# Smaller TensorE matmuls in a recurrent attention kernel: every step padded to 1024 TensorE instructions

## The chip, the core and the metric

The kernel runs on one core of a Trainium2 chip. The core has five engines with instruction streams of their own: TensorE (matmul; the profile calls it PE and its weight loads PEld), VectorE (DVE), ScalarE (ACT), GpSimd (POOL) and SyncE (SP, which here only issues transfers). Transfers run on 16 DMA engines. Data lies in SBUF (128 partitions); matmul results go to PSUM, eight banks of 128 x 512 float32. The metric is the device time of one execution in microseconds (us). Before the change it is 2299.75 us, the median of three runs (2299.54 to 2310.22).

## What is computed

```python
def _A_ref(x, mem0, Wq, Wk, Wv, Wo, seg_len):       # x: (1, 2048, 1024), seg_len 32, 32 heads of 128
    ...
    mem = mem0                                       # 8 memory rows
    for s in range(n_seg):                           # 64 segments
        h = jnp.concatenate([mem, xs], axis=1)       # 8 + 32 rows
        q, k, v = (jnp.einsum('btd,dhe->bhte', h, W) for W in (Wq, Wk, Wv))
        scores = jnp.where(mask, jnp.einsum('bhqe,bhke->bhqk', q, k) * scale, -1e9)
        o = jnp.einsum('bhqk,bhke->bhqe', softmax(scores), v)
        o = jnp.einsum('bhte,hed->btd', o, Wo)
        mem = o[:, :M, :]                            # the first 8 rows are the next segment's memory
        outs.append(o[:, M:, :])
    ...
def _B_ref(x, w_gate, w_up, w_down):
    return _gelu(x @ w_gate) * (x @ w_up) @ w_down
g = sigmoid((x * gate_w).sum(-1, keepdims=True))
out = g * _A_ref(...) + (1 - g) * _B_ref(...)        # bfloat16
```

The 64 segments depend on each other through `mem`, so attention is a chain of 64 steps. The feed-forward part does not depend on it.

## The kernel before

The program first transposes `x` and starts the first projections, then runs the 64 steps of the recurrence (to about 1632 us), and then does the output projection of the rows that no later step needs and the feed-forward part.

In a step, a projection works with only 32 rows: the 8 memory rows and the first 24 rows of the segment. The other 8 rows of a segment depend on nothing earlier, so they are projected for four segments at once ("fill"). A projection piece multiplies a 128 x 32 block of the rows (the weights of the array) by a 128 x 2048 piece of `Wk`, `Wq` or `Wv`. It is issued as four matmuls of 512 columns, each on its own 32 columns of the array and its own 32 partitions of one PSUM bank; the four run side by side. A projection of 16 heads (half of all heads, `u` is 0 or 1) is eight pieces, so 32 matmuls. The weights do not fit into SBUF in full: some pieces share a slot, and `spent` issues the load of the next piece for a slot behind the matmuls that used it up.

The order of all work is written out by hand. `walk` lists the pieces in the order `k0, (second half of the old step's o1), q0, v0, k1, q1, o0, v1, (first half of o1)`, where 0 and 1 are the two halves of the heads. `plan(s)` hangs the other work of a step before certain pieces with `on(m, r, n, ...)`. TensorE executes its stream in exactly this order. Semaphores are derived from reads and writes by `_Prog`; an operation that has to wait for several things gets separate wait instructions ahead of it.

What the change touches and the prediction names:

- `mask` puts the causal mask into the bank of the scores by a matmul of the identity with the mask (L687). It is issued twice in a step, behind the transposes (`trans`, L673) of `q`.
- `scores` (L700) adds the 32 score matmuls; VectorE and ScalarE do the softmax and VectorE transposes the result into `tAB`.
- `attend(u)` multiplies by `v`: `f` is 16 matmuls with the 32 rows' `vA` (L729), `f2` four matmuls with the 8 rows' `vB` (L737). Then ScalarE and VectorE copy the result to `oT`. `attend(ua)` stands behind `q1`, before `o0`; `attend(ub)` stands behind `v1`.
- `fill(m, u, b)` gives eight functions, one for each piece of a projection of the other rows (L841). A step has up to two such projections: `f1` in parts of 3, 3 and the rest around `v1` and `attend(ub)`, `f2` four pieces before and four pieces behind `next_mem(s, 0)`.
- A step without a second fill calls `warm(5)` and `warm(2)` there: matmuls whose result nobody reads (L851).
- `fold` (VectorE) and `next_mem` (two transposes, L825, and a VectorE copy into `hT`) make the next step's memory rows. `next_mem(s, 0)` gives what the first pieces of the next step's `k0` read.
- `o0` (L787) and `o1` (L804) are the output projection of the step.

In the steady part a step has 955 to 979 TensorE instructions, when each matmul is counted as a weight load and a matmul, and each separate wait as one.

## Time and profile before

| what | value |
|---|---|
| median of three runs | 2299.75 us |
| profiled execution | 2308.1 us, span 2306.3 us |
| granted TensorE clock in it | 0.983 |
| TensorE matmuls in the program | 33852 |
| TensorE instructions, matmuls counted twice and with 484 waits and a few others | 68192 |
| recurrence, 125 to 1632 us | 1507 us, TensorE busy 1395.27 us, DMA share 0.93, 333 GB/s |
| the rest, 1632 to 2306 us | 674 us, TensorE busy 661.52 us, DMA share 0.42, 137 GB/s |

A line of the profile's groups reads: line of the kernel, engine, operation, output tile <- input tiles, shapes, count, then busy time and mean duration, then the idle time of the engine just before these instructions and what ended it. "issue" as the thing that ended it means that the profile shows nothing that the engine waited for. A line of a timeline begins with start and length in microseconds; its idle time stands in brackets at the end. Matmuls that run side by side overlap, so mean durations of one matmul are longer than the distance from start to start. The profile shows TensorE's instruction stream as a DMA queue of its own kind, "instruction".

### The profile page before, as it was taken

The numbers are of one execution on the slowest core, as the hardware profiler recorded it, in microseconds if no ns is written. First come the engines' busy times: TensorE is split into PE (matmuls) and PEld (weight loads), VectorE is DVE, ScalarE is ACT, GpSimd is POOL, SyncE is SP. The second block draws the span as 40 slices with busy tenths as digits, with TensorE's granted clock in tenths as the row PEclk, the third lists the DMA queues.
The fourth block names the chain that finished last, engine by engine and source line by source line (L and its number), as shares of the span: only waits on it lengthen the run. The fifth ranks groups of instructions, "written<-read, shape, count | busy, mean of one in ns | idle before, by whom it ended". The sixth has DMA issues, their size and how long they took to land.

```text
span 2306.3 us, 74586 instructions
## 1 busy us (share of the span) xinstructions
PE 2119.9 (92%) x33852; PEld 1048.7 (45%) x33852; DVE 1028.8 (45%) x2440; ACT 541.4 (23%) x1111; POOL 423.7 (18%) x821
## 2 busy tenths in 40 slices
PE   4598999999999999999999999998899999999999
PEld 2244444444444444444444444444464444444444
DVE  3343444454444444544444444454316446163462
ACT  1122222222222222222222222221113123032130
POOL 4422212222222222222222222221100000000000
PEclk8799999999999999999999999999899999999999
DMA  9989999898998999999989899999964440903520
GB/s 375 354 298 327 334 341 358 321 354 320 327 330 325 340 336 316 344 325 355 332 325 354 312 331 341 317 340 324 342 204 143 150 151 10 291 20 125 172 87 19
DMA packets 237579, 638.34 MB, mean 277 GB/s; under 512 B 22440, under 2 KB 91304, under 8 KB 230480
## 3 DMA queue, kind: packets, MB, share of 16 engines
q1 hardware_dynamic: 213440, 596.58, 72.4%
q0 software_dynamic: 13888, 26.31, 3.5%
q10 hardware_dynamic: 9936, 10.69, 1.4%
q8 instruction: 266, 4.36, 0.8%
q14 instruction: 49, 0.40, 0.0%
HBM read 596.85 MB, written 36.63 MB: 275 GB/s over the span
## 4 chain that ended last, share of the span: by engine, by line
PE 70%; DMA 19%; issue 4%; DVE 4%; ACT 2%; POOL 1%; ACTq 0%; SPq 0%; POOLq 0%
PE pb L771 23%; PE pb L1077 15%; DMA sl<-in_A_Wv_dram 7%; PE pb L1131 5%; PE pb L841 5%; PE pb L804 4%; PE pb L787 4%; PE pb L673 3%; DMA qkr<-qk_scr 3%; PE pb L1027 3%; PE pb L1112 2%; PE pb L851 2%; DMA wall<-wg_scr 2%; DMA xr_scr<-xr 1%; DMA o_scr<-oRc 1%
## 5 line engine op out<-in xcount | busy, mean ns | idle before, releaser
L771 PE MATMUL pb<-sl,hT 128*32 128x512 bf16 x12288 | 778.4, 383 | 28.8 <-issue 16.9
L771 PEld LDWEIGHTS pb<-sl,hT 128*32 128x32 bf16 x12288 | 337.5, 97 | 331.6 <-issue 50.8
L841 PE MATMUL pb<-sl,hR 128*32 128x512 bf16 x3072 | 225.3, 392 | 4.1 <-issue 3.2
L1077 PE MATMUL pb<-xT,wg 128*128 128x512 bf16 x896 | 211.7, 379 | 0.7
L1077 PE MATMUL pb<-xT,wu 128*128 128x512 bf16 x896 | 211.7, 379 | 0.0
L804 PE MATMUL pb<-wall,oT 128*32 128x256 bf16 x4056 | 150.9, 275 | 22.9 <-issue 8.5
L787 PE MATMUL pb<-wall,oT 128*32 128x512 bf16 x2048 | 152.4, 387 | 17.1 <-issue 9.5
L656 ACT ACTIVATE kS<-pb 128x512 bf16<-128x512 f32 x127 | 75.8, 597 | 384.3 <-PE pb L771 364.9
L815 DVE COPY part<-pb 64x256 f32<-64x256 f32 x128 | 54.0, 422 | 247.9 <-PE pb L804 246.9
L754 POOL COPY oRc<-oT 128x128 bf16<-128x128 bf16 x128 | 96.4, 753 | 359.2 <-DVE oT L659 357.0
L1131 PE MATMUL pb<-wd,GT 128*128 128x512 bf16 x672 | 146.0, 379 | 1.7 <-DMA wd<-in_B_w_down_dram 1.7
L1085 ACT ACTIVATE s<-pb 128x512 f32<-128x512 f32 x112 | 66.8, 596 | 311.9 <-PE pb L1077 311.9
L708 ACT ACTIVATE E<-pb 128x320 bf16<-128x320 f32 x128 | 55.9, 437 | 352.9 <-DVE pb L707 352.9
L1077 PEld LDWEIGHTS pb<-xT,wg 128*128 128x128 bf16 x896 | 87.2, 98 | 108.0 <-DVE GT L1093 3.7
L1077 PEld LDWEIGHTS pb<-xT,wu 128*128 128x128 bf16 x896 | 87.7, 98 | 105.7
L804 PEld LDWEIGHTS pb<-wall,oT 128*32 128x32 bf16 x4056 | 100.6, 96 | 74.9 <-ACT oT L656 25.9
L1086 DVE SCALAR_TENSOR_TENSOR tp<-s,pb 128x512 f32<-128x512 f32 x112 | 77.0, 687 | 124.2 <-ACT s L1085 124.0
L659 DVE CAST oT<-pb 128x160 bf16<-128x160 f32 x256 | 76.5, 320 | 111.7 <-PE pb L737 111.7
L659 DVE COPY kT<-pb 128x512 bf16<-128x512 bf16 x128 | 54.4, 425 | 159.8 <-PE pb L673 159.5
L880 POOL COPY kT<-qkr 128x128 bf16<-128x128 bf16 x128 | 37.3, 291 | 466.3 <-DVE kT L659 222.6
L841 PEld LDWEIGHTS pb<-sl,hR 128*32 128x32 bf16 x3072 | 82.3, 98 | 70.7 <-issue 20.8
L1090 DVE SCALAR_TENSOR_TENSOR tp<-tp,pb 128x512 f32<-128x512 f32 x112 | 77.1, 688 | 78.6 <-ACT tp L1089 78.6
(100 smaller groups left out, 2286.8 us busy)
## 6 DMA issues: line engine op xcount, KB each, us to landing
sl<-in_A_Wv_dram SPq DMA_DIRECT2D x128, 1024.0 KB, 10.8
wall<-wg_scr SPq DMA_DIRECT2D x53, 1536.0 KB, 9.2
sl<-in_A_Wk_dram SPq DMA_DIRECT2D x64, 1024.0 KB, 5.9
sl<-in_A_Wq_dram SPq DMA_DIRECT2D x64, 1024.0 KB, 9.0
wall<-wo_scr SPq DMA_DIRECT2D x120, 512.0 KB, 6.0
wd<-in_B_w_down_dram SPq DMA_DIRECT2D x42, 1024.0 KB, 5.4
sl<-in_A_Wv_dram SPq DMA_DIRECT2D x75, 512.0 KB, 11.1
wall<-in_A_Wo_dram SPq DMA_DIRECT2D x41, 512.0 KB, 7.9
```

The source lines that it names most:

```text
L656: op("act", lambda e: e.activation(o, i, ACTF.Copy), rd=rd, wr=wr)
L659: op("dve", lambda e: e.tensor_copy(o, i), rd=rd, wr=wr, after=after)
L673: ins = e.transpose(PBV[bank][:, j * 128:(j + 1) * 128], st[:, j * 128:(j + 1) * 128], ident[:, :])
L754: op("pool", lambda e: e.tensor_copy(oRc[:, :, 16 * u:16 * u + 16].rearrange("p c x -> p x c"), oT[:, :, :, 32:40].rearrange("p g j c -> p ...
L771: ins = e.matmul(PB[bk][32 * g:32 * g + 32, :], lhsT=h[:, i, :], rhs=w[:, g * 512:(g + 1) * 512], start=(n == 0), stop=(n == 7))
L787: ins = e.matmul(PB[XO][32 * g:32 * g + 32, :], lhsT=oT[:, j, x, 0:32], rhs=wall[:, na:nb + 1:nb - na, c:c + 256], start=(n == 0 and hp == 0),
L804: ins = e.matmul(PB[XO][32 * g:32 * g + 32, 256 * b:256 * b + 256], lhsT=oT[:, j, x, 0:32], rhs=w[:, c:c + 256], start=False, stop=(n % 4 ...
L841: ins = e.matmul(PB[b][32 * g:32 * g + 32, :], lhsT=h[:, k[2], :], rhs=w[:, g * 512:(g + 1) * 512], start=(n == 0), stop=(n == 7))
L1077: ins = e.matmul(PB[bk][:, 0:FB], lhsT=w[:, kc, cc:cc + 128], rhs=xT[:, :, :, kc, :].rearrange("p t i c -> p (t i) c"), start=(kc == 0), s ...
L1086: op("dve", lambda e, hg=hg, t=t: e.scalar_tensor_tensor(out=t[:, :], in0=s1[:, :], scalar=1.0, in1=hg, op0=ALU.add, op1=ALU.mult), rd=[BK ...
L1090: op("dve", lambda e, hu=hu, t=t: e.scalar_tensor_tensor(out=t[:, :], in0=t[:, :], scalar=1.0, in1=hu, op0=ALU.add, op1=ALU.mult), rd=[BK( ...
L1131: ins = e.matmul(PB[bank[2 * k + hf]][:, :], lhsT=GT[:, j, tb * 128:(tb + 1) * 128], rhs=w[:, jj, hf * 512:(hf + 1) * 512], start=(j == 0) ...
```

## The change

The functions compute the same; some of them issue more, smaller matmuls.

- `mask` is issued as four matmuls on 32 columns of the array each, in place of one on 128. With `last=2` the last of the four is cut into two of half the columns. The mask before `scores(ua)` is called with `last = 1 + ua`, so it has five matmuls in every second step.
- `attend` gets `parts`: its `f2` goes over the four `j` in `parts` groups. `attend(ub)` has `parts=4`, so 16 matmuls of 16 columns in place of 4 of 64. The `attend(ua)` of step 0 has `parts=2`.
- `fill` gets `halves`: the pieces named there are issued as eight matmuls of 256 columns in place of four of 512. `f1` has one such piece for `k` and `q` and two for `v`; `f2` has none.
- `warm` gets `halves` too; one piece of each call is halved.

In all there are 35660 TensorE matmuls in place of 33852. In the steady part four steps together have 4096 TensorE instructions, counted as above, in place of 3868. The number of waits (484) stays, and the other engines' instructions stay as they are.

```diff
-        def mask():
-            op("pe", lambda e: e.matmul(PB[SS][:, 0:320].rearrange("p (a c) -> p a c", a=4), lhsT=ident[:, :],
-                                        rhs=mS[:, :].unsqueeze(1).to_broadcast([128, 4, 80]), start=True, stop=False,
-                                        skip_group_check=True), rd=[ident.r(), mS.r()], wr=[BK(SS)])
+        def mask(last=1):
+            def f(e):
+                for g, a, z in [(0, 0, 4), (1, 0, 4), (2, 0, 4)] + [(3, a, a + 4 // last) for a in range(0, 4, 4 // last)]:
+                    r = slice(32 * g, 32 * g + 32)
+                    ins = e.matmul(PB[SS][r, 80 * a:80 * z].rearrange("p (a c) -> p a c", c=80), lhsT=ident[:, r],
+                                   rhs=mS[:, :].unsqueeze(1).to_broadcast([128, z - a, 80]), start=True, stop=False, skip_group_check=True)
+                return ins
+            op("pe", f, rd=[ident.r(), mS.r()], wr=[BK(SS)])
...
-        def attend(u, by=((2, "act"), (3, "dve"), (0, "act"), (1, "dve")), b3=SS):
+        def attend(u, by=((2, "act"), (3, "dve"), (0, "act"), (1, "dve")), b3=SS, parts=1):
...
             def f2(e):
-                for g in range(4):
-                    r = slice(32 * g, 32 * g + 32)
-                    ins = e.matmul(PB[bo[g]][:, 0:4 * LQ].rearrange("p (j c) -> p j c", j=4)[:, :, 24:40], lhsT=vB[r, u, :],
-                                   rhs=tAB[r, 256:512].rearrange("p (j x) -> p j x", j=4)[:, :, 24:40],
-                                   start=False, stop=True, skip_group_check=True)
+                for js in [slice(j, j + 4 // parts) for j in range(0, 4, 4 // parts)]:
+                    for g in range(4):
+                        r = slice(32 * g, 32 * g + 32)
+                        ins = e.matmul(PB[bo[g]][:, 0:4 * LQ].rearrange("p (j c) -> p j c", j=4)[:, js, 24:40], lhsT=vB[r, u, :],
+                                       rhs=tAB[r, 256:512].rearrange("p (j x) -> p j x", j=4)[:, js, 24:40],
+                                       start=False, stop=True, skip_group_check=True)
                 return ins
...
-        def fill(m, u, b, h=hR):
+        def fill(m, u, b, h=hR, halves=()):
...
-                    for g in range(4):
-                        ins = e.matmul(PB[b][32 * g:32 * g + 32, :], lhsT=h[:, k[2], :], rhs=w[:, g * 512:(g + 1) * 512],
-                                       start=(n == 0), stop=(n == 7))
+                    for c in ((0, 256), (256, 512)) if n in halves else ((0, 512),):
+                        for g in range(4):
+                            ins = e.matmul(PB[b][32 * g:32 * g + 32, slice(*c)], lhsT=h[:, k[2], :], rhs=w[:, g * 512 + c[0]:g * 512 + c[1]],
+                                           start=(n == 0), stop=(n == 7), skip_group_check=True)
...
-        def warm(n):
+        def warm(n, halves=0):
             def f(e):
-                for x in range(4 * n):
-                    g = x % 4
-                    ins = e.matmul(PB[B0][32 * g:32 * g + 32, :], lhsT=hR[:, 7, :], rhs=spare[:, g * 512:(g + 1) * 512],
-                                   start=True, stop=True)
+                for x in range(n):
+                    for c in ((0, 256), (256, 512)) if x < halves else ((0, 512),):
+                        for g in range(4):
+                            ins = e.matmul(PB[B0][32 * g:32 * g + 32, slice(*c)], lhsT=hR[:, 7, :], rhs=spare[:, g * 512 + c[0]:g * 512 + c[1]],
+                                           start=True, stop=True, skip_group_check=True)
...
+        HALF1 = {"k": (6,), "q": (6,), "v": (5, 6)}
+        HALF2 = ()
+        WARM = (1, 1)
...
-            f1 = fill(*fl[0][:2], A1) if fl else []
-            f2 = fill(*fl[1][:2], B0) if two else []
+            f1 = fill(*fl[0][:2], A1, halves=HALF1[fl[0][0]]) if fl else []
+            f2 = fill(*fl[1][:2], B0, halves=HALF2) if two else []
...
-                on("v", 0, 5, mask)
+                on("v", 0, 5, lambda: mask(1 + ua))
...
-                on("k", 1, 1, lambda: attend(ua))
+                on("k", 1, 1, lambda: attend(ua, parts=2))
...
-            on("o", 1, 0, lambda: attend(ub))
+            on("o", 1, 0, lambda: attend(ub, parts=4))
...
-            on("k", 0, 0, some(f2, 4) if two else lambda: warm(5), **nx)
+            on("k", 0, 0, some(f2, 4) if two else lambda: warm(5, WARM[0]), **nx)
             on("k", 0, 0, lambda: next_mem(s, 0), **nx)
-            on("k", 0, 0, some(f2, 4) if two else lambda: warm(2), **nx)
+            on("k", 0, 0, some(f2, 4) if two else lambda: warm(2, WARM[1]), **nx)
```

The lines of the changed kernel that answer to those of before: L771 is L776, L841 is L847, L851 is L858, L825 is L830, L687 is L690, L700 is L704, L729 is L733, L737 is L742, L787 is L792, L804 is L809.

## The prediction

> **What bounds the kernel now.** I read the page first, then the waits of TensorE's weight loads, the timeline at single places, and the busy time by stretches.

> ```profile
> PE 2119.9 (92%) x33852; PEld 1048.7 (45%) x33852; DVE 1028.8 (45%) x2440; ACT 541.4 (23%) x1111; POOL 423.7 (18%) x821
> DMA  9989999898998999999989899999964440903520
> q8 instruction: 266, 4.36, 0.8%
> ```

> TensorE is busy for 92% of the span, and up to 1632 us, where the recurrence ends, the DMA engines are hardly idle either. The last line is the one for this change: 266 packets of 16 KB that carry TensorE's own instructions. 68,192 instructions (each matmul is a weight load and a matmul, and there are 484 separate waits) make 266 packets of 256.

> ```profile
> PEld pb L771 <- issue: 50.8, 126, 2.4
> PEld pb L787 <- issue: 25.1, 79, 2.5
> PEld pb L804 <- issue: 24.1, 33, 2.7
> PEld pb L729 <- issue: 23.6, 57, 0.9
> PEld pb L841 <- issue: 20.8, 48, 2.9
> ```

> "issue" is time in which the engine waited for nothing that the profile shows (columns: total us, times, longest). I numbered TensorE's instructions in program order and laid the starts of the trace on them. The long gaps stand at one remainder modulo 256, so at the borders of the instruction packets. Here is one:

> ```profile
> 540.75 0.40 PE L771 MATMUL pb<-sl,hT 128*32 128x512 bf16 x3
> 543.09 1.90 PE L771 MATMUL pb<-sl,hT 128*32 128x512 bf16 x29 [1.95 <-issue]
> ```

> TensorE stops for 2.3 us in the middle of a group of four. In the trace's list of transfers the packet for this border moves from 540.73 to 541.80, and work resumes 1.29 later. I call the stretch from one `next_mem(s, 0)` to the next a stretch; 54 of them hold 204 borders. Their gaps, less the streaming of the matmul before, add to 68.9 us (1.28 a stretch); 52 are over 0.5 us, the longest is 2.56. At those 52 the packet had landed 1.24 to 1.62 us (median 1.39) before TensorE went on: a packet is usable about 1.35 us after landing. How late it starts depends on the DMA backlog. Mostly that is 3 to 5 us after the border before it, but only about 1.1 us in the one lull of a stretch:

> ```profile
> 1212.20:1218.20 6.00, 5.90 (x141) 2.99 (x138) 4.06 (x12) 1.62 (x5) 1.27 (x3) 1.00 1.03 403
> 1218.20:1221.20 3.00, 2.91 (x84) 1.58 (x83) 1.01 (x5) 1.69 (x4) 1.12 (x2) 1.00 1.05 441
> 1221.20:1225.20 4.00, 3.88 (x76) 1.91 (x72) 0.99 (x3) 0.43 (x1) 2.38 (x5) 1.00 0.71 234
> 1225.20:1230.00 4.80, 4.80 (x92) 2.27 (x84) 1.45 (x4) 1.02 (x3) 1.32 (x2) 1.00 0.97 297
> ```

> The last two columns are the DMA share and GB/s. The third line is the turn of a step (`next_mem`, then the new step's first projections): the loads asked for so far are done, and the next ones wait for TensorE to use up its pieces. Do the gaps cost anything? Over the 54 stretches, length against the sum of gaps has slope 0.85 (correlation 0.77) and intercept 23.1 us, with a mean length of 24.2. So gaps cost 0.85 x 1.28 = 1.09 us a stretch now.

> **The change, part by part.** Four stretches had 971, 979, 963 and 955 TensorE instructions; they get 4096 in all, so borders stand at four places that repeat. By counting the changed program from the same remainder, for steps 4 to 59: A, in the fill or warm-up right behind `next_mem(s, 0)`; B, the first group of `v` between the two `trans`; C, the eighth of 16 matmuls of `attend(ua)`; D, the 26th or 27th of the 32 matmuls of the second `v` projection.

> The added matmuls themselves. Mask, fill halves and warm-up halves stream the same columns: four matmuls of 512 columns on four column tiles start 0.216 us after the four before, four of 256 (L804) 0.109. Two halves are 0.218, so 0.00. Masks: one of 128x320 becomes four tiles side by side that stream the same 320 columns; the 0.1 us of idle that now follows it before the 32-column L771 can only move ahead of it; I take 0, between -0.1 and +0.1 for each of 126 masks. `f2` in `attend(ub)`: 4 matmuls become 16. The 16 of L729 take 0.126 us up to the next line, the 4 of L737 0.14 with a hand-over that stays; so 12 times 6.6 ns = 0.08 us, x63 = +5 us. TensorE waits for nothing new there, and DVE and ScalarE behind it get `oT` 0.08 later. [...]

> The gaps, place by place. Two stretches of before already have borders almost there, those that begin at 1199.20 and 1416.20: gaps of 0.08 and 0.72 at A, 0.01 and 0.06 at B, 0.02 and 0.02 at C, 0.11 and 0.34 at D. B is safe: its packet is asked for in the lull, starts 1.1 us behind A and is usable at 3.5, while A to B takes 6.3 to 6.9. C: usable 4.8 to 5.2 behind B, distance 5.4: 0.05 for the few late ones. For D and A the distance before the border shrinks, because the fillers take instructions but no time, and most of them stand between D and A (24 of `f2`, 8 or 16 of the fill, and half a warm-up). D to A holds only 208 to 224 of the old instructions, about 5.0 us. Here is the second stretch:

> ```profile
> 1433.87 1.70 PE L771 MATMUL pb<-sl,hT 128*32 128x512 bf16 x28
> 1435.91 0.73 PE L771 MATMUL pb<-sl,hT 128*32 128x512 bf16 x4 [0.34 <-DMA sl<-in_A_Wv_dram]
> 1436.27 1.02 PE L841 MATMUL pb<-sl,hR 128*32 128x512 bf16 x12
> ...
> 1440.16 0.23 PE L825 MATMUL pb<-ident,a_bf 64*128 64x64 bf16 x2
> 1440.32 0.61 PE L851 MATMUL pb<-sl,hR 128*32 128x512 bf16 x8
> 1440.76 1.47 PE L771 MATMUL pb<-sl,hT 128*32 128x512 bf16 x24
> 1442.70 0.51 PE L804 MATMUL pb<-wall,oT 128*32 128x256 bf16 x12 [0.47 <-issue]
> ```

> D would stop at about 1435.3; its packet landed at 1434.84 and was usable at about 1436.2. That is 0.9 late, but the wait for the last `v` piece, which ends at 1435.91, lies right behind and covers most: net 0.35. Over the ten stretches with a border within 40 instructions of C and none in between, D's packet would be 0.46 late on average (0.99 without moving its request back to C); behind the cover I take 0.25 net, between 0 and 0.6. A stands at 1440.4, behind L825. The packet asked for at 1436.26 moved from 1440.18 to 1441.27 and was used at 1442.70 (the border was then in L771): it would be 2.2 late. Over 18 stretches with a border within 52 instructions of D it would be 1.66 late on average (0.4 to 3.0), or 0.94 if each request is moved back to D's place. D itself will resume late, so the truth lies between: I take 1.35. Nothing covers A: the DMA engines are running dry there, the next loads wait for the pieces behind A, and `hT` is ready by then.

> Sum for a stretch: 1.35 + 0.25 + 0.05 = 1.65 against 1.09 now, +0.56. Times 56 stretches +31, and `f2` +5: **+36 us**. The profiled execution was 2308.1 us (span 2306.3, clock 0.983), 8.4 above the 2299.75 median; added to the median that is **2336 us**, and about 2344 in a profile. With A and D at their low ends (0.94 and 0) the change is about zero, with 1.66 and 0.6 it is +73: the forecast's own range is 2312 to 2372, where the low end is the border of "slower".

> **The rivals.**
> *The four places are good ones: faster.* Borders within 12 instructions of the four places lose 0.23, 0.04, 0.02 and 0.28, together 0.57 a stretch, the least of 16 offsets I tried. Effective 0.85 x 0.57 = 0.48, saving 0.61 x 56 = 34, less 5: 2271 us. Against it: in those borders the request before A was made about 45 instructions earlier than D will be. It decides if A's packet starts under 2.7 us behind D instead of 3.9, the value in both stretches above; for that the backlog at D must be a third smaller.
> *Nothing to gain or lose.* Four borders at the present mean of 0.34 lose 1.35 instead of 1.28: with `f2` 2299.75 + 3 + 5 = 2308. A milder A of about 0.9 gives the same. [...]
> *The lull makes A worse: much slower.* With few gaps elsewhere TensorE reaches D with the DMA backlog grown by up to the 0.7 us it no longer loses, so A waits 2.0 and D's cover is late too: 2.7 a stretch, +90 + 5, 2395 us.
> *The borders are not where I count them*, because what runs ahead of the program differs: any offset is possible, mean as in the second rival.

> **How the numbers follow.** Forecast 0.60; the faster rival 0.25; nothing to gain or lose 0.10, with the shifted borders in it; much slower 0.05. About 0.5%, 11.5 us, can be told from no change. Of the forecast 0.02 falls under that: faster 0.25, same 0.12, slower 0.63. The range goes from 2268, which holds half of the faster rival, to 2372, which leaves out the much slower one.

> **What would show it.** "issue" gaps of 0.9 to 2 us behind L830 in most stretches, at one place, with a packet that starts 3.5 to 4.5 us behind the border in the second `v` projection; nearly none between the two `trans` and in `attend(ua)`; at D gaps under 1 us; the 16 matmuls of L742 started within 0.15 us. If A's gap is under 0.5, the prediction is wrong and the kernel is faster; if the gaps of a stretch add to 1.3 again but spread, the borders are not pinned. If the loads of L809 wait longer, the saved time became a wait for DMA.

## The result

The changed kernel takes 2327.59 us (median of 4, 2326.37 to 2338.07), the kernel before beside it 2300.83 (median of 4, 2299.54 to 2310.22): a ratio of 1.0117 with a 95% interval of 1.0078 to 1.0157. It is 27 us slower; 36 were forecast. Its profiled execution took 2327.23 us (span 2325.4, granted clock 0.985), 19.1 more than that of before, which lay 7 us above its kernel's median. Medians and ratios below leave out two executions that took over 1.5% more than the fastest of their kernel: 2420.98 us in the run with 16 short matmuls, and 2340.3 in the run with 40 behind A.

The page of the changed kernel, the lines that were shown of before (line numbers are its own from here on):

```profile
PE 2136.7 (92%) x35660; PEld 1116.2 (48%) x35660; DVE 1028.9 (44%) x2440; ACT 538.6 (23%) x1111; POOL 422.9 (18%) x821
DMA  9999998998988989889988889989965350803520
q8 instruction: 280, 4.59, 0.8%
```

14 more packets of instructions (280 for 266), and no other engine works more. 2 x 35660 instructions and 484 waits over 280 packets are 256 a packet. Numbered in program order, the steps from start to start over every 256th instruction add to 133 us at one remainder, and to no more than 42 at any other but its two neighbours. TensorE's busy time grew by 16.8 us; the pair of kernels without a backlog, below, has nearly the same growth (2101.1 against 2086.3) at 6 us more time, so busy time is not where the 27 us can be read. The DMA engines have the same data to move (596.58 MB in the largest queue, before and now) and are no busier (71.0% of the span in that queue, 72.4% before). From the waits of the weight loads (total us, times, longest):

```profile
PEld pb L776 <- issue: 49.4, 72, 1.4
...
PEld pb L847 <- issue: 40.5, 54, 2.0
...
PEld pb L858 <- issue: 38.1, 26, 2.3
...
PEld pb L733 <- issue: 21.5, 53, 1.3
...
PEld pb L776 <- DMA sl<-in_A_Wv_dram: 9.1, 17, 1.2
...
PEld pb L809 <- issue: 6.5, 13, 1.3
```

What was spread over many lines now stands at two fillers: L847 and L858, where A lies, have 78.6 us of "issue"; L841 and L851 had 23.2 before. The scattered ones at L809 fell from 24.1 to 6.5. The wait for the pieces of `v` fell from 24.2 to 9.1. All "issue" lines of the weight loads together did not grow (182.3 us before, 176.7 now), so this view tells where TensorE stops, and not how much longer; that is read from the starts at the borders, below.

One turn of a step in the timeline of TensorE (start, us, instructions, idle before):

```profile
664.70 1.69 PE L776 MATMUL pb<-sl,hT 128*32 128x512 bf16 x26
666.78 0.61 PE L776 MATMUL pb<-sl,hT 128*32 128x512 bf16 x6 [0.39 <-issue]
667.01 1.03 PE L847 MATMUL pb<-sl,hR 128*32 128x512 bf16 x16
668.08 0.27 PE L733 MATMUL pb<-tAB,vA 32*128 32x40 bf16 x16
668.19 0.25 PE L742 MATMUL pb<-tAB,vB 32*128 32x16 bf16 x16
668.37 0.62 PE L847 MATMUL pb<-sl,hR 128*32 128x256 bf16 x12
668.94 1.06 PE L809 MATMUL pb<-wall,oT 128*32 128x256 bf16 x32
669.82 1.26 PE L858 MATMUL pb<-sl,hR 128*32 128x256 bf16 x24
671.01 0.23 PE L830 MATMUL pb<-ident,a_bf 64*128 64x64 bf16 x2
671.17 0.29 PE L858 MATMUL pb<-sl,hR 128*32 128x256 bf16 x3
673.08 0.61 PE L858 MATMUL pb<-sl,hR 128*32 128x256 bf16 x9 [1.62 <-issue]
673.42 1.56 PE L776 MATMUL pb<-sl,hT 128*32 128x512 bf16 x24
```

D is the second line, after 26 of 32 matmuls: a stop of 0.39. A is the line at 673.08: three matmuls of the warm-up have run, then TensorE stands for 1.62 us. In the list of transfers the packet for A starts at 670.61, 3.83 us behind D's border, ends at 671.63, and work resumes 1.45 us after that. The stretches around it (length, then busy time of PE, PEld, DVE, ACT, POOL with counts, clock, DMA share, GB/s):

```profile
661.50:667.50 6.00, 5.54 (x126) 2.97 (x122) 3.82 (x11) 0.91 (x5) 1.26 (x3) 1.00 1.05 391
667.50:670.50 3.00, 2.96 (x110) 1.99 (x106) 0.98 (x3) 1.57 (x4) 1.29 (x3) 1.00 1.02 434
670.50:674.50 4.00, 2.38 (x47) 1.62 (x42) 0.59 (x2) 0.00 (x0) 2.16 (x4) 1.00 0.40 115
674.50:679.30 4.80, 4.80 (x101) 2.92 (x93) 1.02 (x3) 0.60 (x1) 1.10 (x2) 1.00 0.83 237
```

The third line has A's stop in it: the DMA engines moved 115 GB/s after 391 and 434 in the lines ahead of it. So A's packet moves as the last of a backlog, and TensorE then stands while the DMA engines run dry: it frees no pieces, so no loads start (SyncE issues none of weights between 663.86 and 674.15). A's stop isn't what makes the lull: a kernel below, whose stop at this place is 0.29 by its timeline, has 114 GB/s in the 4 us around its packet for A.

A gap is counted from start to start over a border, less the streaming of the matmul before it, so it is a little longer than the idle time in a timeline's brackets (1.79 against 1.62 for the A above). Over the same 54 stretches the gaps at borders now add to 93.3 us, 1.73 a stretch (1.28 before); 71 of 216 are over 0.5 us. The mean stretch is 24.72 us (24.22 before). By place, as means:

| place | gap, us | over 0.5 | from the border before, us | packet starts after that border, us |
|---|---|---|---|---|
| A | 1.10 | 46 of 54 | 5.02 | 3.79 |
| B | 0.05 | 0 of 54 | 6.74 | 1.23 |
| C | 0.13 | 1 of 54 | 5.42 | 2.08 |
| D | 0.45 | 24 of 54 | 5.45 | 3.53 |

### The profile page after: what moved, and what is told of

The parts are those of the page before. It is cut to its first block, busy times and chain, and to the rows that moved or that the text cites. A ratio compares the mean times of both kernels' runs of the same rounds, so it can differ in the third digit from the quotient of the medians.

```text
span 2325.4 us, 78202 instructions
## 1 busy us (share of the span) xinstructions
PE 2136.7 (92%) x35660; PEld 1116.2 (48%) x35660; DVE 1028.9 (44%) x2440; ACT 538.6 (23%) x1111; POOL 422.9 (18%) x821
## 3 DMA queue, kind: packets, MB, share of 16 engines
q1 hardware_dynamic: 213440, 596.58, 71.0%
## 4 chain that ended last, share of the span: by engine, by line
PE 75%; DMA 13%; issue 5%; DVE 4%; ACT 1%; POOL 1%; ACTq 0%; SPq 0%; POOLq 0%
PE pb L776 26%; PE pb L1087 14%; PE pb L847 6%; PE pb L1141 5%; PE pb L809 5%; DMA sl<-in_A_Wv_dram 5%; PE pb L792 4%; PE pb L673 3%; PE pb L1037 2%; PE pb L858 2%; PE pb L1122 2%; PE pb L733 1%; DMA xr_scr<-xr 1%; PE pb L704 1%; DMA qkr<-qk_scr 1%
## 5 line engine op out<-in xcount | busy, mean ns | idle before, releaser
L776 PE MATMUL pb<-sl,hT 128*32 128x512 bf16 x12288 | 793.5, 383 | 23.3 <-issue 18.3
L776 PEld LDWEIGHTS pb<-sl,hT 128*32 128x32 bf16 x12288 | 375.5, 97 | 292.9 <-issue 49.4
L847 PE MATMUL pb<-sl,hR 128*32 128x512 bf16 (+1 forms) x3428 | 233.9, 367 | 21.1 <-issue 20.4
L809 PE MATMUL pb<-wall,oT 128*32 128x256 bf16 x4056 | 152.3, 276 | 10.2 <-DMA wall<-in_A_Wo_dram 5.0
L792 PE MATMUL pb<-wall,oT 128*32 128x512 bf16 x2048 | 149.6, 387 | 6.6 <-issue 0.6
L847 PEld LDWEIGHTS pb<-sl,hR 128*32 128x32 bf16 x3428 | 93.4, 98 | 91.3 <-issue 40.5
L809 PEld LDWEIGHTS pb<-wall,oT 128*32 128x32 bf16 x4056 | 110.5, 97 | 46.4 <-ACT oT L656 22.9
```

The costliest lines, as they stand in the source:

```text
L776: ins = e.matmul(PB[bk][32 * g:32 * g + 32, :], lhsT=h[:, i, :], rhs=w[:, g * 512:(g + 1) * 512], start=(n == 0), stop=(n == 7))
L792: ins = e.matmul(PB[XO][32 * g:32 * g + 32, :], lhsT=oT[:, j, x, 0:32], rhs=wall[:, na:nb + 1:nb - na, c:c + 256], start=(n == 0 and hp == 0),
L809: ins = e.matmul(PB[XO][32 * g:32 * g + 32, 256 * b:256 * b + 256], lhsT=oT[:, j, x, 0:32], rhs=w[:, c:c + 256], start=False, stop=(n % 4 ...
L847: ins = e.matmul(PB[b][32 * g:32 * g + 32, slice(*c)], lhsT=h[:, k[2], :], rhs=w[:, g * 512 + c[0]:g * 512 + c[1]], start=(n == 0), stop=( ...
```

## The experiments

The theory: a packet is asked for when the border before it is crossed, waits its turn behind the weight loads, takes about 1.05 us to move and is usable 1.4 us after that; TensorE stops when it comes to the border sooner. (The asking itself is not in the profile. In the fourteen traces 2953 of 2965 packets start behind the first matmul past the border before, and the other 12 up to 1.4 us ahead of it.) So the change costs what A and D cost, by where they lie and by the way before them. Rivals: the added matmuls cost time themselves; pinning the borders, wherever, costs it; a border costs a fixed time, whatever the DMA engines do; or A's packet is late since the lull is there, whatever the way before it. The way to a border is the time from the border before it to the last matmul ahead of it.

**Shift all borders of the changed kernel.** 64 or 16 short matmuls, once, in step 0:

```diff
+        def pad(n):
+            def f(e):
+                for x in range(n):
+                    g = x % 4
+                    ins = e.matmul(PB[B0][32 * g:32 * g + 32, 0:64], lhsT=hR[:, 7, :], rhs=slots[home["q", 0, 7]][:, 0:64],
+                                   start=True, stop=True, skip_group_check=True)
+                return ins
+            op("pe", f, rd=[hR.r(224), slots[home["q", 0, 7]].r()], wr=[BK(B0)])
...
                 on("k", 1, 1, lambda: attend(ua, parts=2))
+                on("k", 1, 1, lambda: pad(64))
```

> The changed kernel with 64 small matmuls (128 TensorE instructions, some 1 us) added once in step 0, so that in every later step the four packet borders stand 128 instructions earlier in the work; nothing else differs. Theory (a border costs what its packet is late, and that depends on where in the step it was asked for): the borders now ask at other backlogs; replayed with the packet delays of the two traces the gaps fall from 1.73 us a stretch to 0.9 to 1.2, so 2280 to 2305 us, about 2290. Rival (the added small matmuls themselves cost the time): they are all still there, so 2328 to 2330, and the gaps stay in L742, L690 and the halved fills.

> As before, but 16 small matmuls (32 instructions) in step 0. Theory: this is the worst of the offsets in the replay, 2.6 to 3.4 us of gaps a stretch, so 2365 to 2405 us. Rival (the small matmuls): 2328. Rival (any repeated offset is as good as another, the fifth-of-a-percent more packets cost the time): 2320 to 2335 as well.

With 64: 2307.67 us, ratio 1.0036 (1.0015 to 1.0057), gaps 1.17. The gaps fell as expected, the time to 3 us above the expected range: with gaps a little under those of before the kernel is still slower than before, so a small part of the change's cost isn't in the gaps. With 16: 2399.88 us, ratio 1.0465 (1.041 to 1.052), both as expected, gaps 2.96, nearly all at two places: 1.43 in the second `v` projection, whose packet starts 4.38 us behind the border before, and 1.53 in the last matmuls ahead of A's old place, with a way of only 4.60 us before it. Its waits:

```profile
PEld pb L776 <- issue: 111.9, 83, 2.6
PEld pb L847 <- issue: 54.3, 57, 2.6
PEld pb L858 <- issue: 53.0, 32, 2.6
```

One program, apart from some matmuls in step 0, spans 92 us by the place of its borders alone. A fixed price of pinning, or of the small matmuls, is excluded as the main cause.

**The control: the same pad in the kernel before.** 16 matmuls, where the borders wander.

> The kernel before with 16 short matmuls (32 instructions) more in step 0, so every later border stands 32 instructions earlier in the code, as in the run where that cost the changed kernel 73 us. Control for the padding itself. Theory: without 1024 to a step the borders wander through all places anyway, so an offset changes nothing: gaps 1.2 to 1.35 us a stretch, 2295 to 2308 us, ratio within 0.4% of before. Rival (the pad itself, or where the program's first packets end, costs the time): ratio over 1.01.

2302.02 us, ratio 0.9989 (0.9969 to 1.0009), gaps 1.21. The pad itself costs nothing that can be told.

**The instructions without the pinning.** All masks cut into seven matmuls, which makes 1035 instructions a stretch, so that borders wander again:

```diff
-                on("v", 0, 5, lambda: mask(1 + ua))
+                on("v", 0, 5, lambda: mask(4))
...
-                on("o", 0, 2, mask)
+                on("o", 0, 2, lambda: mask(4))
```

> The changed kernel with the last column tile of both masks cut into four, 6 more matmuls in an even step and 5 in an odd one less what the change had: 1035 instructions a step, so the borders drift through all places and are not pinned. Theory: what counts beside the place is that fillers without time bring the borders closer in time (6.0 us against 6.4); averaged over all places 1.7 to 2.1 us a stretch, so 2322 to 2348 us, about 2333, not faster than the pinned kernel. Rival (pinning at these four places is what made the change slow): the gaps go back to the 1.3 us a stretch of the kernel before, 2303 to 2312 us.

2353.6 us, ratio 1.0224 (1.0193 to 1.0255), gaps 2.17 a stretch (1.7 to 2.1 expected): 6 us over the expected range, and over 40 above the rival's. That the borders stand still is not what costs; 1035 instructions that wander are worse than 1024 that stand at A to D. The named reason, more instructions in the same time bring borders closer in time, fits the time per border (a stretch less its gaps, divided by its borders: 6.1 us before, 5.75 in the changed kernel, 5.7 here). But a run below has 5.7 with gaps of 1.22, so that is not the whole of it.

**Take the backlog away.** The loads that bring each `v` piece back are left out, first in the changed kernel, then in the kernel before (the projections of `v` then use what lies in the slot):

```diff
-            if nk is not None:
+            if nk is not None and (mv or nk[0] != "v"):
...
-                if any(mv for _, _, mv in q) or (k[0] == "o" and not all(nk in kept for _, nk, _ in q)):
+                if k[0] == "v" or any(mv for _, _, mv in q) or (k[0] == "o" and not all(nk in kept for _, nk, _ in q)):
```

> The changed kernel without the reloads of the v pieces that share a slot (five of the fourteen 512 KB reloads of a step; the second half of the heads then uses the first half's Wv pieces, so the output is another). The TensorE stream is the same. Theory (packets are late because the DMA engines are backlogged): packets start 1 to 2 us behind the border before, gaps under 0.3 us a stretch in sum, 2235 to 2262 us. Rival (a border costs TensorE or its sequencer a fixed time, whatever the DMA engines do): gaps of 1.1 us at A and 0.45 at D stay, and the time falls only by the waits for v pieces, under 10 us: 2318 to 2328.

> The kernel before, without the loads that bring each v piece back while the recurrence runs (the same edit as in the lean run of the changed kernel, so the output isn't the reference's; everything else is issued as before). Tells whether the changed kernel's extra time needs the DMA backlog. Theory (packets wait behind data): with the backlog gone the gaps go in this kernel too, from 1.28 us a stretch to 0.3 to 0.6, and both lean kernels take about the same: 2222 to 2238 us, the 5 us of the 12 more f2 matmuls less than the lean changed kernel's 2231, gaps aside. Rival (the added small matmuls cost time themselves, in the PE queue): the lean before is still some 25 us under the lean changed kernel, 2200 to 2210 us.

The lean changed kernel took 2231.32 us (one run), the lean before 2225.24 (median of 4, 2222.01 to 2228.48). From the page of the lean changed kernel, and its waits:

```profile
DMA  9868777667676776767667666666870721704420
```

```profile
PEld pb L858 <- issue: 16.8, 24, 2.1
...
PEld pb L847 <- issue: 13.2, 36, 1.5
...
PEld pb L776 <- issue: 9.3, 28, 2.1
```

The DMA share over the recurrence is 0.69 (0.90 with the loads), A's two lines fall from 78.6 to 30.0 us and L776's from 49.4 to 9.3. The packet starts 1.76 us behind the border before it in the mean (2.66 with the loads), gaps are 0.49 a stretch, and 0.26 in the lean before. By place A's gap fell from 1.10 to 0.34 and D's from 0.45 to 0.00, so a border has no fixed price. Expected were gaps under 0.3 and at least 2235 us in the lean changed kernel, and gaps of 0.3 to 0.6 in the lean before; all three were missed by a little. The change, with all its added matmuls, then costs some 6 us in place of 27. That is one run against four that spread over 6.5 us, and it holds the difference in gaps too, so the price of the matmuls themselves is a few us at most.

**How deep may the backlog be?** On the kernel before, a weight load is issued only when the third (or second) load before it has landed:

```diff
+        ld = []
+
+        def load(fn, **kw):
+            ld.append(op("sp", fn, after=ld[-3:][:1] if len(ld) >= 100 else [], **kw))
...
-                op("sp", lambda e: e.dma_start(dst(t, k), src(k)), wr=[t.r()], lane=lane)
+                load(lambda e: e.dma_start(dst(t, k), src(k)), wr=[t.r()], lane=lane)
...
```

> The kernel before, but from the hundredth load of a weight piece on, SyncE issues a load only when the third load before it has landed, so at most three (512 to 1536 KB each) are under way instead of as many as there are free slots. Same bytes. Tells whether a packet of instructions is late because of the depth of the backlog or only because the DMA engines are busy. Theory (depth): a packet starts 2 to 3 us behind the border before it instead of 3.2, gaps 0.6 to 1.1 us a stretch instead of 1.28, and the time is 2260 to 2295 us, unless the loads come too late. Rival (busy is enough): start 3.2 and gaps 1.2 to 1.3 as before, 2296 to 2310. Side effect to watch: waits of TensorE for pieces (v, o) that come late; if they grow by over 1 us a stretch the time is over 2330.

> The same with two loads under way. Theory (depth): packet start 1.5 to 2.5 us, gaps 0.2 to 0.7 us a stretch, but two loads of 512 KB are only 2.4 us of transfer at 430 GB/s while one needs 5 to 6 us from issue to landing when alone in the queue with others, so the loads themselves come late and the sum is open: 2250 to 2400 us. Rival (busy is enough): gaps 1.2 to 1.3, and no gain from this at any depth.

With three: 2368.62 us, ratio 1.0285 (1.0254 to 1.0316). With two: 2514.34, ratio 1.0935 (1.091 to 1.0961). The gaps did fall, to 0.64 and 0.43, and the packets start 2.96 and 2.49 us behind the border instead of 3.32, all within what depth had asked for. But the way between borders grew with the stretch (25.23 and 27.47 us), which makes gaps smaller by itself, and both times are longer than expected. A wait of TensorE with three under way:

```profile
PEld pb L809 <- DMA wall<-wg_scr: 66.0, 41, 3.6
```

It was 4.8 us in the kernel before. So the side effect decides the time, and depth against mere business stays open: the packet's start moved, by 0.36 and 0.83 us, but so did the pace at which TensorE asks for loads.

**Put the added instructions elsewhere.** Mask, `f2`, `fill` and `warm` as in the kernel before. Instead, 31, 22, 27 or 34 matmuls (by `s % 4`) of the projections right behind A, in the lull, go as two halves:

```diff
+        CUTS = [("k", 0, 0), ("k", 0, 1), ("k", 0, 2), ("k", 0, 3), ("q", 0, 0), ("q", 0, 1), ("q", 0, 2), ("q", 0, 3), ("k", 0, 4)]
+        CUT = (31, 22, 27, 34)
...
+                cut = max(0, min(4, CUT[s % 4] - 4 * CUTS.index((m, r, n)))) if s and (m, r, n) in CUTS else 0
...
-                    for g in range(4):
-                        ins = e.matmul(PB[bk][32 * g:32 * g + 32, :], lhsT=h[:, i, :], rhs=w[:, g * 512:(g + 1) * 512],
-                                       start=(n == 0), stop=(n == 7))
+                    for c in ((0, 256), (256, 512)) if cut else ((0, 512),):
+                        for g in range(4):
+                            if g < cut or c[0] == 0:
+                                c1 = c[1] if g < cut else 512
+                                ins = e.matmul(PB[bk][32 * g:32 * g + 32, c[0]:c1], lhsT=h[:, i, :], rhs=w[:, g * 512 + c[0]:g * 512 + c1],
+                                               start=(n == 0), stop=(n == 7), skip_group_check=True)
...
+                on("k", 1, 1, lambda: pad(30))
```

> The kernel with the added instructions behind A, its offset chosen (30 short matmuls in step 0) so that A stands where it stands in the changed kernel, within 8 instructions. Mask, f2, fill and warm are as before, so D to A holds 256 old instructions instead of 208 to 224, and the border ahead of A stands some 40 instructions earlier in the second v projection. Theory (A's packet is late since the fillers shorten the way from D to A by a us): distance ahead of A 5.7 to 6.2 us instead of 5.0, and A's gap falls from 1.10 to 0.3 to 0.6 us, while the border ahead of it may take what it saves (0.3 to 1.6). Rival (the place, right before the DMA lull, makes A's packet late whatever the distance): gap at A 0.9 or more again. The time isn't what tells them apart: 2295 to 2340 us.

This run has A at the same place with a longer way to it. Its timeline, in the same stretch as above (L779 are the projections, L849 and L859 the fillers):

```profile
667.13 0.60 PE L779 MATMUL pb<-sl,hT 128*32 128x512 bf16 x6
669.48 1.69 PE L779 MATMUL pb<-sl,hT 128*32 128x512 bf16 x26 [1.74 <-issue]
...
674.69 0.23 PE L833 MATMUL pb<-ident,a_bf 64*128 64x64 bf16 x2
674.85 0.61 PE L859 MATMUL pb<-sl,hR 128*32 128x512 bf16 x7
675.75 0.39 PE L859 MATMUL pb<-sl,hR 128*32 128x512 bf16 x1 [0.29 <-issue]
```

A's stop, the last line, is 0.29 instead of 1.62; over all stretches A's gap is 0.40 (1.10 in the changed kernel). The way to A is 5.88 us (5.02) and the packet starts 3.97 behind the border (3.79), no sooner. So the place and the lull are not the cause of A's gap: the shortened way is. The border behind A, in the lull, had a way of under 5 us before it, as short as A's in the changed kernel, and no gap (0.00). The border ahead of A now stands after 6 matmuls of the `v` projection instead of 26 and lost 1.45; the sum was 1.92 and the time 2334.47 us, ratio 1.0165 (1.0125 to 1.0204).

The same kernel at three other offsets:

> 1024 instructions a step in the mean, but the added ones elsewhere: mask, f2, fill and warm as in the kernel before, and 31, 22, 27 or 34 matmuls of the first k and q projections (right behind A, in the lull, where packets come at once) go as two halves. 72 short matmuls in step 0 set the offset. Theory: the distances before D and A keep their time, gaps add to 0.6 to 1.0 us a stretch against 1.28 before, and the time is 2268 to 2295 us, about 2280: faster than both kernels. Rival (1024 to a step is no gain at any offset, since the sum over places stays): gaps 1.2 or more, 2300 to 2330.

> The same with 40 short matmuls in step 0 instead of 72, so borders stand 64 instructions later: one of them has 0.7 us of gap there and the other three nearly none. Theory: gaps 0.8 to 1.2 us a stretch, 2275 to 2302 us, about 2288, some 5 to 10 above the run with 72. Rival (offset decides little here): both equal within 4 us.

> The same with 80 short matmuls in step 0, 16 instructions earlier than in the fastest run so far (72). Theory: the optimum is flat, gaps 0.9 to 1.3 us a stretch, 2280 to 2298 us, again faster than the kernel before by 0.2 to 0.9%. Rival (the run with 72 was a lucky place): 2300 us or more.

With 72: 2291.35 us (median of 10), ratio 0.9951 (0.9929 to 0.9973): faster than both kernels. With 80: 2293.19, ratio 0.9966 (0.9942 to 0.9991). With 40: 2309.86, ratio 1.0026 (0.9994 to 1.0059), outside what was expected, though its profiled execution took 2294.03 with gaps of 1.02: its executions go from 2290.77 to 2318.69, and why they differ so much stays open. The gaps of the first two (1.22 and 1.32) missed their forecast and are hardly below the 1.28 of before, so the gain of 0.3 to 0.5% isn't shown to come from them.

All runs together, from the profiled executions (54 stretches each; "pad" is the number of short matmuls in step 0, "lean" is without the loads of `v`). The last column is what the line of the kernel before, 23.1 + 0.85 x gaps, gives:

| kernel | gaps, us a stretch | packet starts after border, us | stretch, us | by the line |
|---|---|---|---|---|
| before | 1.28 | 3.32 | 24.22 | 24.19 |
| changed | 1.73 | 2.66 | 24.72 | 24.57 |
| changed, pad 64 | 1.17 | 3.18 | 24.33 | 24.09 |
| changed, pad 16 | 2.96 | 3.14 | 25.61 | 25.62 |
| changed, masks cut further | 2.17 | 3.12 | 25.09 | 24.94 |
| before, pad 16 | 1.21 | 3.25 | 24.21 | 24.13 |
| behind A, pad 30 | 1.92 | 3.35 | 24.78 | 24.73 |
| behind A, pad 40 | 1.02 | 2.86 | 24.05 | 23.97 |
| behind A, pad 72 | 1.22 | 3.31 | 24.06 | 24.14 |
| behind A, pad 80 | 1.32 | 3.43 | 24.33 | 24.22 |
| changed, lean | 0.49 | 1.76 | 23.20 | 23.52 |
| before, lean | 0.26 | 2.22 | 23.15 | 23.32 |

The line was fitted within one execution of before; it tells the stretch of kernels with very different borders within 0.25 us where the loads are as before, and within 0.32 in the lean ones. The two paced kernels are off it by 1.6 and 4.0 us: their loads come late. Each row is a single execution. Those of before, pad 72 and pad 80 behind A took 7 to 14 us more than the medians of their kernels, those of pad 16 in the changed kernel and pad 40 some 16 less, so a row's gaps need not be those of the median.

## Why the prediction was right

- *Where the borders stand.* As counted: A, B, C and D, in each of the 54 stretches. That they might not be where I count them is out.
- *A.* 1.35 was forecast, 1.10 measured. The way from D to A was 5.0 in the forecast and 5.02 measured; the start behind D 3.9 and 3.79. The middle of the two bounds (0.94 and 1.66) that the forecast took for a D that resumes late was somewhat too high. A's gap splits by step: 0.86 where a `fill` lies behind `next_mem` (L847) and 1.33 where the warm-up does (L858). The experiment with the way restored shows the named reason, fillers that take instructions but no time.
- *D.* 0.25 net was forecast. The gap is 0.45, and the wait for `v` pieces beside it fell by 15.1 us, which is 0.27 for each of 56 stretches, so about 0.18 net. That the wait fell because of D is argued from its place, not tested.
- *B and C.* 0 and 0.05 forecast, 0.05 and 0.13 measured. C still has 0.10 and B its 0.05 in the lean kernel, where their packets are in time, so this part isn't lateness.
- *Sum.* Gaps of 1.73, less the 0.27 of `v`, are 1.46 against an effective 1.09 before: +0.37, where 0.56 was forecast. The stretch grew by 0.50. `f2` has 0.04 of the difference and the masks 0.02; the other 0.07 a stretch (4 us in all) is not assigned. The recurrence, all 62 stretches, went from 1506.6 to 1528.5 us, and what lies around it was 2.8 shorter, which is the 19.1 between the two profiles.
- *Masks and halves.* 0 was forecast. From the transposes ahead of a mask to the matmul behind it 0.473 us pass, 0.463 before, so 0.02 a stretch. A warm-up of 24 matmuls takes 1.19 us, as the one of 20 did, so these fillers take no time.
- *`f2`.* 16 matmuls start within 0.085 us, and the next line starts 0.18 after the first of them (0.14 with 4): 0.04 x 63 = 2.5 us, where I had 5. The starts are 6 ns apart.
- *The rivals.* The faster one asked for A's packet under 2.7 us behind D; that was so in 2 of 54 stretches. For the much slower one A would have to wait 2.0 us; it waits 1.10. "Nothing to gain or lose" needed gaps of 1.35, and they are 1.73; by the offset alone the changed kernel takes 2307.67 or 2399.88 us, so the places do count. In the lean kernels, with gaps of 0.26 to 0.49 us, they can count for less.
- *Luck.* The mechanism and the two places were right; how near the sum came is in part luck. The forecast counts the coming gaps in full (1.65), but those of before at 0.85. At 0.85 throughout it is 0.31 a stretch and 2322 us; the measured gaps give 0.85 x 1.73 - 1.09 = 0.38, or 21 us. The profiles, on which all gaps rest, differ by 19.1 us, about half of the 36; the medians differ by 27, since the profiled execution of before was 7 us longer than its kernel's median.
- *The loads.* L809 would have waited longer if saved time had become a wait for DMA. The opposite came: its waits for loads are smaller. That a slower TensorE asks later would explain it; no run tests it.

```profile
L809 PE MATMUL pb<-wall,oT 128*32 128x256 bf16 x4056 | 152.3, 276 | 10.2 <-DMA wall<-in_A_Wo_dram 5.0
```

The idle time ahead of these matmuls was 22.9 us before, with the same loads as 7.5 of it.

## What to carry to other kernels

In this kernel TensorE's own instructions come late where it works on short matmuls while the DMA engines are full of weights (at A: 5.02 us from the border before, 434 GB/s ahead of it, a gap of 1.10). To look for the same elsewhere, number the instructions, lay them on the trace and see whether the long "issue" gaps stand at one remainder modulo 256. What counts at a border is the time that the 256 instructions before it take, against the start of the packet plus some 2.45 us (here 1.05 to move and 1.4 from landing to use); so instructions that take no time belong ahead of a border whose packet comes quickly, as in the lull (B's after 1.23 us), and not ahead of one that waits behind a backlog (A's after 3.79). Single borders show this (A with 1.10 against 0.40, the one behind it with 0.00); a gain in time from it isn't shown, for the runs that did so took from 2291 to 2334 us by their offset. Once the number in a loop is a multiple of 256, one offset holds for the whole loop: try several, since here 16 matmuls in the first step were worth 72 us.
